# Attention with locality-sensitive hashing, then two feed-forward blocks: product with v in runs of three key blocks

## The chip, the cores and the metric

The kernel runs on one core of one Trainium2 chip. The metric is the device time of the program in microseconds; the smaller the better. The profile is of one execution, and its times count from the first instruction (the span).

## The reference

Inputs: q, k, v of shape (2, 8, 768, 64), `proj` (64, 6), and the weights of two feed-forward blocks. Everything is float32.

```python
q_bucket = sum over bits of ((q @ proj) > 0) * 2**bit      # k_bucket in the same way
mask = q_bucket[:, :, :, None] == k_bucket[:, :, None, :]
scores = where(mask, (q @ k.T) / sqrt(64), -1e9)
attn = exp(scores - max) / (sum + 1e-9)
x = (attn @ v), heads side by side                          # 1536 tokens x 512
h = x @ w_in;  x = (h * cos(h)) @ w_out                     # w_in 512 x 2048
out = (silu(x @ w_gate) * (x @ w_val)) @ w_out2             # w_gate, w_val 512 x 1536
```

## The kernel before

The instructions are issued in the order in which the program writes them; each engine has its own queue and works it off in that order, and waits on semaphores where data or a buffer is missing.

Attention works on 8 pairs of heads (`NPAIR`), two heads j = 0, 1 side by side. A pair has 6 blocks of 128 queries, so there are 48 units u (`NU`); three units make a half of the queries of a pair (384 queries), 16 halves (`NH`). The loop at L701 calls `att_step(u)` for each unit, and L723, L724 and L733 call it for five more steps (u = 48 to 52) in which the last units drain. One step works on three ages of units at once:

- for unit u: `mm_scores(u, j)` (L458) makes the scores of 128 queries against 768 keys: two matmuls over X and Y (L466) and two over Z and W (L468), which carry the hash bits and the low parts, into a PSUM tile `s` (two buffers). `row_max` (L471) on VectorE takes the tile to SBUF as `p` with its row minimum of the negated scores, `row_exp` (L482) on ScalarE makes the exponentials and their sums;
- for unit u - 1: `row_norm` (L491): VectorE makes the reciprocal `rv` of the sums (L493, L494) and POOL multiplies both `p` with it (L497);
- for unit u - 2: `p_transpose(u - 2, j, g, engine)` (L501), four times, for head j and half g of the keys: three 128x128 transposes on TensorE (L510) into a PSUM tile `t`, of which there are two (`ps_t`, L218), and one copy of the three into `pt`, by ScalarE (L516) in the calls (0, 0), (1, 0) and (1, 1), by VectorE (L518) in the call (0, 1);
- for a half whose three units are transposed: `av(half, kb)` (L522): the product of v with `pt` for key block kb = 0 to 5, one matmul for each head (L528), accumulated in the one PSUM tile `av` (`ps_v`). Each of these float32 matmuls shows as two instructions of 384 columns; v has 64 columns, so head 0 takes one half of the array's columns and head 1 the other. `av_close(half)` (L534) copies the finished tile to `xh` on ScalarE (L539) and puts what is left of it in `xl` on VectorE (L540).

In step u, `hv, kv = divmod(u - 5, HB)` with `HB` = 3 names the half and which of its three steps this is. Key blocks 2 kv and 2 kv + 1 come behind the first two calls of `p_transpose`, and `av_close` comes in the third step ahead of the last two calls.

In between, `fill("prep")` and `fill("build")` (L602) move two side jobs on by one piece. `prep` (L273) prepares q and k of the next pair in the first three units of a pair: transposes (L286), their copies (L292 on ScalarE, L296 on VectorE), casts (L300), the hash bits (L329, L335, L339), the low parts on POOL (L356), and the DMAs that place them, all on SP's queue. `build_early` (L169) takes one weight chunk of 64-bit floats to float32 in nearly every third unit: one copy on ScalarE (L137) and three steps on VectorE (L152, L156, L160).

After attention the first feed-forward block (L1055 on) and the second (L1111 on) run, with nearly all matmuls in `each_of_three` (L644).

Of the kernel before, what the change touches and what calls it, by code (L numbers as in the profile page):

```python
# [26 lines left out]
def lsh_attention_moe_moe2(  # L27
# [20 lines left out]
    NBLK = S // P  # L48
    HALF = S // 2
    HB = NBLK // 2  # L50
# [407 lines left out]
    def mm_scores(u, j):  # L458
        pr, i = divmod(u, NBLK)
        X, Y, Z, W = heads[pr]  # L460
        ps = ps_s.tile([P, 1024], F32, tag="s", name=f"s{u}_{j}")
        KZ = D + 2 * NB
        qs = slice(i * P, (i + 1) * P)
        cols = (slice(0, 512), slice(512, S))
        for ks in cols:
            nc.tensor.matmul(out=ps[:, ks], lhsT=X[:, j, qs], rhs=Y[:, j, ks], start=True, stop=False)  # L466
        for ks in cols:
            nc.tensor.matmul(out=ps[:, ks], lhsT=Z[:KZ, j, qs], rhs=W[:KZ, j, ks], start=False, stop=True)  # L468
        scores[u, j] = ps

    def row_max(u, j):  # L471
        ps = scores.pop((u, j))
        pt = pp.tile([P, S], F32, tag="p", name=f"p{u}_{j}")
        mn = sm.tile([P, 1], F32, tag="mn", name=f"mn{u}_{j}")
        nc.vector.tensor_scalar(  # L475
            out=pt, in0=ps[:, :S], scalar1=-MASKED, scalar2=None,
            op0=ALU.min, op1=ALU.min, accum_out=mn,
        )
        probs[u, j] = pt
        nbias[u, j] = mn  # L480

    def row_exp(u, j):  # L482
        pt = probs[u, j]
        if j == 0:
            sums[u] = sm.tile([P, 2], F32, tag="sv", name=f"sv{u}")
        nc.scalar.activation(  # L486
            out=pt, in_=pt, func=AF.Exp, bias=nbias.pop((u, j)), scale=-1.0,
            accum_out=sums[u][:, j : j + 1],
        )

    def row_norm(u):  # L491
        rv = sm.tile([P, 2], F32, tag="rv", name=f"rv{u}")
        nc.vector.tensor_scalar(out=rv, in0=sums.pop(u), scalar1=EPS, scalar2=None, op0=ALU.add)  # L493
        nc.vector.reciprocal(out=rv, in_=rv)  # L494
        for j in range(2):
            pt = probs[u, j]
            nc.gpsimd.tensor_scalar(  # L497
                out=pt, in0=pt, scalar1=rv[:, j : j + 1], scalar2=1.0, op0=ALU.mult, op1=ALU.mult
            )

    def p_transpose(u, j, g, eng):  # L501
        half, i = divmod(u, HB)
        if (half, j) not in pts:
            pts[half, j] = pv.tile([P, NBLK, HALF], F32, tag="pt", bufs=4, name=f"pt{half}_{j}")
        dst = pts[half, j]
        src = probs[u, j]
        ps = ps_t.tile([P, 512], F32, tag="t", name=f"t{u}_{j}_{g}")
        for c in range(HB):
            kb = g * HB + c
            nc.tensor.transpose(  # L510
                ps[:, c * P : (c + 1) * P], src[:, kb * P : (kb + 1) * P], ident
            )
        o = dst[:, g * HB : (g + 1) * HB, i * P : (i + 1) * P]
        s3 = ps[:, :HALF].rearrange("p (c t) -> p c t", c=HB)
        if eng == "act":
            nc.scalar.activation(out=o, in_=s3, func=AF.Copy)  # L516
        else:
            nc.vector.tensor_copy(o, s3)  # L518
# [3 lines left out]
    def av(half, kb):  # L522
        pr, hf = divmod(half, 2)
        if kb == 0:
            avs[half] = ps_v.tile([P, 512], F32, tag="av", name=f"av{half}")
        ps = avs[half]
        for j in range(2):
            nc.tensor.matmul(  # L528
                out=ps[j * D : (j + 1) * D, :HALF],
                lhsT=nat["v", pr][:, j, BLOCKS[kb], :], rhs=pts[half, j][:, kb, :],  # L530
                start=(kb == 0), stop=(kb == NBLK - 1),
            )

    def av_close(half):  # L534
        pr, hf = divmod(half, 2)
        ps = avs.pop(half)
        b, cc = divmod(pr, H // 2)
        sl = slice(b * S + hf * HALF, b * S + (hf + 1) * HALF)
        nc.scalar.activation(out=xh[:, cc, sl], in_=ps[:, :HALF], func=AF.Copy)  # L539
        nc.vector.tensor_tensor(  # L540
            out=xl[:, cc, sl], in0=ps[:, :HALF], in1=xh[:, cc, sl].bitcast(F32),
            op=ALU.subtract,
        )
        pts.pop((half, 0)), pts.pop((half, 1))
# [54 lines left out]
    NH = NPAIR * 2  # L599
    side = {"prep": iter(()), "build": iter(())}  # L600

    def fill(*what):  # L602
        for nm in what:
            next(side[nm], None)

    def att_step(u):


        hv, kv = divmod(u - 5, HB)
        live = u < NU  # L610
        tr = 0 <= u - 2 < NU
        if live:
            mm_scores(u, 0)
        if 0 <= u - 1 < NU:
            row_exp(u - 1, 1)
        if tr:
            p_transpose(u - 2, 0, 0, "act")
        if live:
            row_max(u, 0)
        if 0 <= u - 1 < NU:  # L620
            row_norm(u - 1)
        fill("prep")
        if tr:
            p_transpose(u - 2, 0, 1, "dve")
        if 0 <= hv < NH:
            av(hv, 2 * kv)
            av(hv, 2 * kv + 1)
        fill("prep", "build")
        if live:
            mm_scores(u, 1)  # L630
            row_exp(u, 0)
        if 0 <= hv < NH and kv == HB - 1:
            av_close(hv)
        if tr:
            p_transpose(u - 2, 1, 0, "act")
        if live:
            row_max(u, 1)
        fill("prep")
        if tr:
            p_transpose(u - 2, 1, 1, "act")  # L640
            probs.pop((u - 2, 0)), probs.pop((u - 2, 1))
        fill("prep", "build")
# [58 lines left out]
    for u in range(NU):  # L701
        pr, i = divmod(u, NBLK)
        if i == 0:
            side["prep"] = prep(pr + 1) if pr + 1 < NPAIR else iter(())
            if pr == 0:
                rest, second = first, side["prep"]
                order = (rest, rest, second, second, second, second, second, rest, rest)
                side["prep"] = itertools.chain((next(g) for g in order), second)
        if i == 4 and pr + 2 < NPAIR:
            load_pair(pr + 2, "qk")  # L710
        if i == 5 and 0 < pr < NPAIR - 1:
            load_pair(pr + 1, "v")
        if u + 3 in early_steps:
            fetch_next()
        if u in early_steps:
            side["build"] = build_early(early_steps.index(u))
        if u >= NU - 5 and u < NU - 1:
            split(*(uses[0] + uses[1] + uses[2])[u - NU + 5], pool=qk, tag="XYZW"[u - NU + 5], bufs=2)
        att_step(u)

    hps[0] = ps_p.tile([P, 512], F32, tag="pp", name="h0")
    side["prep"] = (hidden(hps[0], "in", 0, [a]) for a in range(NCC))
    att_step(NU)  # L723
    att_step(NU + 1)  # L724
    hps[1] = ps_t.tile([P, 512], F32, tag="t", name="h1")
    actx.close()
# [463 lines left out]
```

## Time and profile before

| | |
|---|---|
| device time, median of 3 runs | 797.24 us (795.46 to 798.85) |
| span of the profiled execution | 793.2 us (its own device time is not given apart from it) |
| instructions | 12687 |
| TensorE busy (matmuls) | 775.2 us, 98% |
| VectorE busy | 608.1 us, 77% |
| ScalarE busy | 516.3 us, 65% |
| POOL busy | 498.6 us, 63% |
| av matmuls (L528) | 384 instructions, starting from 35.4 to 252.5 us |

PE is TensorE's matmuls, PEld its weight loads, DVE is VectorE, ACT is ScalarE. The ends of matmuls are modelled and they overlap, so the distance between starts tells more than a length. Idle time of an engine that the others don't wait for costs nothing. A row that merges several instructions (x8) runs from the first one's start to the last one's end.

### The profile page before, as it was taken

To read this page: it belongs to the slowest core of one execution; us is meant where nothing else is said; L and a number is where in the kernel's file an instruction comes from. 1 tells how busy PE (TensorE), PEld (TensorE's weight loads), DVE (VectorE), ACT (ScalarE), POOL (GpSimd) and SP (SyncE) were. 2 spreads that over 40 slices of the span, in tenths; PEclk is the share of its full clock that TensorE was granted. 3 is DMA by queue.
4 is the path that set the end of the run, shared out by engine and by line. 5 is a ranking of instruction groups with operands and counts; after the bars stand their busy time and mean duration, and the time that the engine had idled before them with its cause. 6 is when DMAs were issued, how large, how long until landed. Compare 5 with 4: busy or idle time off the path is not lost. (4 is left out here: it accounts for less than half of the span.)

```text
span 793.2 us, 12687 instructions
## 1 busy us (share of the span) xinstructions
PE 775.2 (98%) x4100; PEld 634.3 (80%) x4100; DVE 608.1 (77%) x1121; ACT 516.3 (65%) x1009; POOL 498.6 (63%) x426
## 2 busy tenths in 40 slices
PE   6799999999999999999999999999999999999998
PEld 4666666666676788888888888889999989999996
DVE  6878888888774899988888799587777687655654
ACT  5778777777885888787778777744444445444432
POOL 4764565466463777767767988657655595655450
PEclk9999999999999999999999999999999999999999
DMA  3755756666413577878875756122122213412102
GB/s 119 192 132 150 202 133 174 173 139 165 126 41 115 181 241 235 263 251 289 294 229 189 254 194 224 40 68 67 54 81 66 80 27 126 141 42 79 41 1 79
DMA packets 72545, 113.01 MB, mean 142 GB/s; under 512 B 6656, under 2 KB 44704, under 8 KB 72480
## 3 DMA queue, kind: packets, MB, share of 16 engines
q1 hardware_dynamic: 72480, 112.21, 46.9%
q8 instruction: 32, 0.52, 0.3%
q14 instruction: 33, 0.27, 0.1%
HBM read 76.29 MB, written 18.35 MB: 119 GB/s over the span
## 5 line engine op out<-in xcount | busy, mean ns | idle before, releaser
L497 POOL TENSOR_SCALAR p<-p,rv 128x768 f32<-128x768 f32 x96 | 94.9, 1000 | 91.7 <-DVE rv L494 64.3
L475 DVE TENSOR_SCALAR_CACHE_REDUCE p<-s 128x768 f32<-128x768 f32 x96 | 91.1, 953 | 31.6 <-PE s L468 27.8
L486 ACT ACTIVATE p<-p,mn 128x768 f32<-128x768 f32 x96 | 89.8, 935 | 9.0 <-DVE p L475 4.9
L516 ACT ACTIVATE pt<-t 128x384 f32<-128x384 f32 x144 | 66.6, 486 | 41.3 <-PE t L510 41.1
L510 PE MATMUL t<-ident,p 128*128 128x128 f32 x576 | 85.0, 273 | 4.5 <-DVE pt L518 4.1
L510 PEld LDWEIGHTS t<-ident,p 128*128 128x128 f32 x576 | 67.5, 140 | 14.5 <-DVE pt L518 4.8
L528 PE MATMUL av<-pt,vn 128*64 128x384 f32 x384 | 72.1, 498 | 0.0
L930 ACT ACTIVATE uh<-u 128x384 fp32r<-128x384 f32 x48 | 23.8, 521 | 62.4 <-DVE u L925 62.4
L466 PE MATMUL s<-Y,X 128*128 128x512 f32 x192 | 58.8, 387 | 1.5 <-DVE X L389 1.5
L685 ACT ACTIVATE r<-r 128x512 f32<-128x512 f32 x48 | 30.4, 633 | 34.8 <-DVE r L677 34.7
L468 PE MATMUL s<-W,Z 76*128 76x512 f32 x192 | 50.2, 343 | 2.6 <-DVE Z L439 2.4
L466 PEld LDWEIGHTS s<-Y,X 128*128 128x128 f32 x192 | 29.0, 191 | 28.5 <-DVE rv L494 7.8
L673 DVE SCALAR_TENSOR_TENSOR rf<-ki,h 128x512 f32<-128x512 int32 x46 | 31.9, 693 | 20.4 <-ACT ki L670 20.0
L919 ACT ACTIVATE sg<-gate 128x384 f32<-128x384 f32 x36 | 18.9, 526 | 42.7 <-DVE gate L970 42.6
L137 ACT ACTIVATE w<-raw 128x512 f32<-128x512 f32 x68 | 44.7, 659 | 1.1 <-DMA raw<-in_moe_w_gate_dram 1.1
L646 PE MATMUL o<-out_1s,uh 128*128 128x512 f32 x144 | 44.9, 392 | 0.0
L646 PE MATMUL o<-out_0s,uh 128*128 128x512 f32 x144 | 44.9, 392 | 0.0
L528 PEld LDWEIGHTS av<-pt,vn 128*64 128x64 f32 x384 | 23.4, 136 | 25.8 <-issue 25.6
L697 DVE TENSOR_TENSOR g<-h,r 128x512 f32<-128x512 f32 x48 | 33.0, 687 | 13.0 <-ACT r L686 13.0
L156 DVE SCALAR_TENSOR_TENSOR bw<-w,bw 128x512 int32<-128x512 int32 x55 | 38.0, 691 | 2.4 <-ACT w L137 1.4
L152 DVE TENSOR_SCALAR bw<-raw 128x512 int32<-128x512 int32 x55 | 37.9, 689 | 0.6
L160 DVE SCALAR_TENSOR_TENSOR w<-raw,bw 128x512 int32<-128x512 int32 x55 | 37.5, 681 | 0.6
(1814 smaller groups left out, 2442.2 us busy)
## 6 DMA issues: line engine op xcount, KB each, us to landing
f<-w SPq DMA_DIRECT2D x58, 256.0 KB
raw<-in_moe_w_out_dram SPq DMA_DIRECT2D x28, 512.0 KB
raw<-in_moe_w_in_dram SPq DMA_DIRECT2D x16, 512.0 KB
raw<-in_moe_w_gate_dram SPq DMA_DIRECT2D x12, 512.0 KB
raw<-in_moe_w_val_dram SPq DMA_DIRECT2D x12, 512.0 KB
Y<-kH SPq DMA_DIRECT2D x28, 192.0 KB
vn<-in_v_dram SPq DMA_DIRECT2D x8, 384.0 KB
gate_0f<-f SPq DMA_DIRECT2D x12, 256.0 KB
```

Source lines behind the costliest of these rows:

```text
L137: nc.scalar.activation(out=t, in_=raws[i][:, :, 1].bitcast(F32), func=AF.Copy, scale=2.0**-112)
L152: nc.vector.tensor_scalar(out=sign, in0=high, scalar1=-(2**31), scalar2=None, op0=ALU.bitwise_and)
L156: nc.vector.scalar_tensor_tensor(out=word, in0=ti, scalar=3, in1=sign, op0=ALU.logical_shift_left, op1=ALU.bitwise_or)
L466: nc.tensor.matmul(out=ps[:, ks], lhsT=X[:, j, qs], rhs=Y[:, j, ks], start=True, stop=False)
L468: nc.tensor.matmul(out=ps[:, ks], lhsT=Z[:KZ, j, qs], rhs=W[:KZ, j, ks], start=False, stop=True)
L475: nc.vector.tensor_scalar(out=pt, in0=ps[:, :S], scalar1=-MASKED, scalar2=None, op0=ALU.min, op1=ALU.min, accum_out=mn,)
L486: nc.scalar.activation(out=pt, in_=pt, func=AF.Exp, bias=nbias.pop((u, j)), scale=-1.0, accum_out=sums[u][:, j : j + 1],)
L497: nc.gpsimd.tensor_scalar(out=pt, in0=pt, scalar1=rv[:, j : j + 1], scalar2=1.0, op0=ALU.mult, op1=ALU.mult)
L510: nc.tensor.transpose(ps[:, c * P : (c + 1) * P], src[:, kb * P : (kb + 1) * P], ident)
L516: nc.scalar.activation(out=o, in_=s3, func=AF.Copy)
L528: nc.tensor.matmul(out=ps[j * D : (j + 1) * D, :HALF], lhsT=nat["v", pr][:, j, BLOCKS[kb], :], rhs=pts[half, j][:, kb, :], start=(kb == 0) ...
L646: nc.tensor.matmul(out=out_ap, lhsT=s, rhs=m, start=first and i == 0, stop=last and i == 2, **flags)
```

## The change

The twelve matmuls of a half are made in two runs in place of three. In the first of the three steps (kv = 0) key blocks 0 to 2 are multiplied, at the old place behind the first two transposes; in the second step (kv = 1) key blocks 3 to 5, behind `row_max(u, 1)` and a piece of `prep`, between the third and the fourth call of `p_transpose`, and `av_close` follows at once. The third step has no product with v.

```diff
         if tr:
             p_transpose(u - 2, 0, 1, "dve")
-        if 0 <= hv < NH:
-            av(hv, 2 * kv)
-            av(hv, 2 * kv + 1)
+        if 0 <= hv < NH and kv == 0:
+            for kb in range(HB):
+                av(hv, kb)
         fill("prep", "build")
         if live:
             mm_scores(u, 1)
             row_exp(u, 0)
-        if 0 <= hv < NH and kv == HB - 1:
-            av_close(hv)
         if tr:
             p_transpose(u - 2, 1, 0, "act")
         if live:
             row_max(u, 1)
         fill("prep")
+        if 0 <= hv < NH and kv == 1:
+            for kb in range(HB, NBLK):
+                av(hv, kb)
+            av_close(hv)
         if tr:
             p_transpose(u - 2, 1, 1, "act")
```

## Rows read from the trace of the kernel before

**Rows 1.** The page, part 1: busy time of each engine, share, instructions.

```profile
PE 775.2 (98%) x4100; PEld 634.3 (80%) x4100; DVE 608.1 (77%) x1121; ACT 516.3 (65%) x1009; POOL 498.6 (63%) x426
```

**Rows 2.** Windows: length; busy us (count) PE, PEld, DVE, ACT, POOL; clock; DMA.

```profile
34.00:232.00 198.00, 197.42 (x1298) 137.40 (x1297) 161.84 (x374) 152.56 (x336) 113.63 (x108) 1.00 0.59 152
```

**Rows 3.** Waits of TensorE, 34 to 232 us: us in total, times, longest.

```profile
PE trq L286 <- DMA qn<-in_q_dram: 0.4, 1, 0.4
PE s L468 <- DMA W<-kT: 0.2, 1, 0.2
```

**Rows 4.** Timeline of TensorE's matmuls, units 27 and 28: start us, us, what.

```profile
139.78 0.82 PE L510 MATMUL t<-ident,p 128*128 128x128 f32 x6
140.53 1.51 PE L528 MATMUL av<-pt,vn 128*64 128x384 f32 x8
141.97 0.62 PE L466 MATMUL s<-Y,X 128*128 128x512 f32 x2
142.43 0.52 PE L468 MATMUL s<-W,Z 76*128 76x512 f32 x2
142.78 0.82 PE L510 MATMUL t<-ident,p 128*128 128x128 f32 x6
143.35 0.61 PE L466 MATMUL s<-Y,X 128*128 128x512 f32 x2
```

**Rows 5.** Timeline of TensorE's matmuls at the end of attention.

```profile
243.32 1.51 PE L528 MATMUL av<-pt,vn 128*64 128x384 f32 x8
244.76 0.88 PE L510 MATMUL t<-ident,p 128*128 128x128 f32 x6
...
248.85 4.09 PE L528 MATMUL av<-pt,vn 128*64 128x384 f32 x24
```

**Rows 6.** Timeline of VectorE, units 27 to 28.

```profile
144.47 0.68 DVE L160 SCALAR_TENSOR_TENSOR w<-raw,w 128x512 int32<-128x512 int32 x1
145.07 0.94 DVE L475 TENSOR_SCALAR_CACHE_REDUCE p<-s 128x768 f32<-128x768 f32 x1
...
145.95 0.16 DVE L493 TENSOR_SCALAR rv<-sv 128x2 f32<-128x2 f32 x1
...
146.22 0.54 DVE L518 COPY pt<-t 128x384 f32<-128x384 f32 x1
147.50 0.56 DVE L540 TENSOR_TENSOR xl<-av,xh 128x384 fp32r<-128x384 f32 x1 [0.74 <-ACT xh L539]
147.97 0.95 DVE L475 TENSOR_SCALAR_CACHE_REDUCE p<-s 128x768 f32<-128x768 f32 x1
```

**Rows 7.** Timeline of ScalarE, units 27 to 28.

```profile
140.62 0.49 ACT L516 ACTIVATE pt<-t 128x384 f32<-128x384 f32 x1
...
147.00 0.47 ACT L539 ACTIVATE xh<-av 128x384 fp32r<-128x384 f32 x1
...
148.96 0.94 ACT L486 ACTIVATE p<-p,mn 128x768 f32<-128x768 f32 x1 [0.41 <-DVE p L475]
```

**Rows 8.** Timeline of VectorE in unit 31, with preparation of the next pair.

```profile
160.47 0.56 DVE L300 CAST qH<-qT 128x768 fp32r<-128x768 f32 x1
160.95 0.55 DVE L296 COPY kT<-trk 128x384 f32<-128x384 f32 x1
```

**Rows 9.** Timeline of all engines in unit 4, a unit without av.

```profile
29.84 0.60 PE L466 MATMUL s<-Y,X 128*128 128x512 f32 x2
...
30.95 1.83 POOL L356 TENSOR_TENSOR kT<-kT,kH 128x768 f32<-128x768 f32 x1
...
31.72 1.09 DVE L493 TENSOR_SCALAR rv<-sv 128x2 f32<-128x2 f32 x1
...
32.92 0.54 DVE L518 COPY pt<-t 128x384 f32<-128x384 f32 x1
...
33.52 0.55 PE L510 MATMUL t<-ident,p 128*128 128x128 f32 x3 [0.95 <-DVE pt L518]
...
33.82 0.60 PE L466 MATMUL s<-Y,X 128*128 128x512 f32 x2
```

## The prediction, made before the change was run

> **What bounds the kernel now.** I read the engine shares first, then the windows by stage, then TensorE's waits, then its order of time inside the attention stage. TensorE is busy nearly all the time [rows 1]. In the stretch that the change touches, 34 to 232 us, it is busy 197.42 of 198 us at the full granted clock, 1.00, which is the 2.4 GHz level [rows 2], and it waits 0.6 us for anybody there, 0.4 for a load of q and 0.2 for W [rows 3]. So the stage runs at the rate at which TensorE can issue. VectorE is busy 161.84 us and ScalarE 152.56 us of the same 198 us [rows 2]: they follow with about a fifth of their time to spare. What the change takes from TensorE's stream shortens the kernel; any wait that it puts there lengthens it. The stages behind it are TensorE's too, so a shift goes through to the end.
>
> A matmul's length is no measure of its cost, since they overlap; I use the distance between starts. Three letters name units u by u mod 3: A (2), B (0), C (1). Before, each has two key blocks of av; afterwards A has three, B three (late, between its last two transposes), C none. S0, S1 are the two score products, T00 to T11 the four groups of three transposes, AV2 and AV3 two and three key blocks for both heads.
>
> **What is removed: changes between av and its neighbours.** Six transposes in front of scores take 142.78 to 143.35, 0.57 us; in front of av 139.78 to 140.53, 0.75. Av then takes until the scores start at 141.97, 1.44 [rows 4]. An AV2 between transposes and scores therefore costs 0.75 + 1.44 - 0.57 = 1.62 us. The same work in one long run is cheaper: 24 matmuls are 4.09 us long, 8 are 1.51 [rows 4, 5], so eight further pairs cost 2.58 us, 0.32 a pair. Four pairs are 1.29 us; the other 0.33 us is the change of kind. An AV3 in that place costs 1.62 + 0.64 = 2.26. Between two transposes (the late place) the trace has one case: av from 243.32, transposes at 244.76, again 1.44, and six transposes 0.88 long in place of 0.82 [rows 5]. It replaces six transposes at 0.11 each: 0.75 + 1.44 + 0.06 - 0.66 + 0.64 = 2.23. Per half: 3 x 1.62 = 4.86 before, 2.26 + 2.23 = 4.49 after, so 0.37 less. The last half's 24 matmuls stand in one run already [rows 5], which leaves 15 halves: 5.5 us saved (5.0 if only 0.33 goes each time).
>
> **What is moved: av_close.** Its copy xh (ScalarE) and difference xl (VectorE) come one unit earlier, behind the late AV3 of B. It issues no DMA and passes nothing on the queues of SP and POOL. But on ScalarE it now stands before B's last copy of transposes and C's first exponential, and on VectorE before the last step of the weight build (L160), C's first row maximum, the reciprocal (rv) and the copy of T01. That an xl holds those behind it is in the trace: VectorE stands idle 0.74 us for xh before the xl at 147.50, and the row maximum behind it starts only at 147.97 [rows 6].
>
> **What then limits C.** T11 can't start until VectorE has copied T01, since the transposes share two PSUM tiles. Time from the end of the late AV3 in B, with the handover of 0.06 us that rows 9 show between such a copy's end (32.92 + 0.54) and the transpose:
> TensorE starts T11 of B at -0.07 (1.44 against 1.51), S0 0.31 later (0.06 + 2 x 0.11 + 0.03), then 0.81 for scores, 0.57 for six transposes, 0.81 for scores [rows 4] and 0.33 for T10: it is ready for C's T11 at 2.76.
> VectorE: xh starts at 0.06 and xl 0.50 behind it (147.00 to 147.50), 0.47 to the next, L160 0.60 (144.47 to 145.07), row maximum 0.88, rv 0.27, copy 0.54 [rows 6, 7]: 3.32, so T11 starts at 3.38 and TensorE stands for 0.62 us. S0 is not late: it starts at 0.24 and is written 0.98 later (0.46 to the second product and its 0.52) [rows 4], before the row maximum at 1.63.
> With the preparation of the next pair (u mod 6 = 1, up to 37) VectorE also casts q, 0.48 from start to start, and copies one transposed k, about as long (0.55 against 0.56), before T01's copy [rows 8]; TensorE has two more groups of three transposes, 0.33 each: 0.62 + 0.96 - 0.66 = 0.92. Without a weight build (u = 40), ScalarE decides: the handover, xh, B's copy of T11 and the exponential that rv waits for, 0.06 + 0.47 + 0.49 + 0.94 [rows 7], let rv start at 1.96 in place of 2.51: 0.07 us.
> Units 7 to 46 hold 14 such C: six with preparation, seven without, one without a build: 6 x 0.92 + 7 x 0.62 + 0.07 = 9.9 us. A and B get longer on TensorE (4.38 to 5.0), which gives the other engines time to catch up; in B, today T10 (142.78) starts 1.67 us after ScalarE's copy of T00 has ended (140.62 + 0.49) with an AV2 between [rows 4, 7]; 1.62 us of that goes, and the 0.05 that is left is the handover, so I count no wait there. At the end, unit 49 has no av between its transposes: T10 waits for ScalarE's copy of T00, about 0.22 + 0.27 + 0.06 + 0.49 + 0.06 = 1.10 us after T00 starts, where two groups of transposes take 0.66: 0.4 us.
>
> The bounds of one such C. Below: nothing, if VectorE's chain overlaps more than its row spacings say; less than nothing is excluded, for TensorE has no wait there to lose. Above: the last unit that ran without av, u = 4, took 3.98 us from S0 to S0 (29.84 to 33.82), where TensorE's own work is 0.81 + 0.57 + 0.81 + 0.57 = 2.76: 1.22 lost, 0.95 of it at the very wait named above, T11 for T01's copy [rows 9]. There rv took 1.09 us and ended with a POOL instruction that began before it (30.95 + 1.83 = 32.78) [rows 9]; elsewhere it takes 0.16 [rows 6]. In the new C no such long POOL instruction stands beside rv, so I keep 0.62 and 0.92.
>
> **The sum.** 9.9 + 0.4 - 5.5 = +4.8 us, on a span of 793.2 us. The profile gives no time of its own for what lies around the span; the median of the runs, 797.24, is 4.0 above it, and I carry that over: 802.0 us.
>
> **The rivals.**
> Faster: the time in C is covered and only the changes of kind count: 797.2 - 5.5 = 791.7 us. It holds where VectorE's copy of T01 ends within 2.76 us of the av run, that is if its six steps take 0.6 us less than their spacing today. For it: VectorE has a fifth of idle time; against it: the steps are one queue, and it starts with a wait. The Trainium skill's "TensorEngine Tiling (Array Packing)", under Key Properties of its Tiling Modes, says that a change of tiling mode, not of the tile alone, drains TensorE. By that rule alone fewer changes are simply faster; the trace has the change at 0.33 us, and no run here shows yet that it is a drain.
> A wash: the waits in C are near 0.35 us each, half of what I reckon, because the chain's steps overlap somewhat: 14 x 0.35 + 0.4 - 5.5, about 797 us.
> Slower by more: C is as long as u = 4, since rv or the casts meet a POOL instruction: 14 x 1.22 + 0.4 - 5.5 = +12.0, 809.2 us. The Trainium skill's "SBUF — State Buffer" (Who interferes with whom) says that VectorE in a two-port mode and GpSimd exclude each other for a whole instruction; the rows with 1.09 us agree [rows 9].
>
> **How the numbers follow.** My forecast (797.5 to 806) gets 0.56, faster 0.14, the wash 0.15, slower by more 0.15. About 0.5%, 4 us, is what a measurement of this kernel can tell from no change. My forecast lies just above that bound: I give two thirds of its chance to slower and a third to no difference. Slower 0.38 + 0.15 = 0.53; same 0.18 + 0.15 = 0.33; faster 0.14. The range, 793 to 809, leaves out the faster case and the far end of the slowest one.
>
> **What would show it.** Right: among TensorE's waits between 34 and 232 us, about 13 for VectorE's copy of T01, 9 to 10 us together, where there are none now; av in runs of 12 matmuls, some 2.15 us long; units from S0 to S0 of about 5.0, 5.0 and 3.4 us, and 4.3 for a C with preparation. Wrong on the saving: the first transposes after the late av start later than 1.44 us after an equal AV2 would allow. Wrong on the wait: no such waits, C at 2.8 us. Wrong on its cause: the waits are for ScalarE's copies (T10) or for scores' PSUM. A C near 4.0 us with rv longer than 1 us would be the last rival.

## The result and the profile after

The changed kernel takes 803.29 us (median of 4 runs, 802.70 to 804.74); the kernel before took 796.88 us beside it (795.46 to 798.85). The ratio is 1.0090, with a 95% interval of 1.0073 to 1.0107: 6.4 us slower, where 4.8 were forecast (802.0 us).

The page's part 1 and the stretch of [rows 2] in the windows view, in the kernel after (columns as there):

```profile
PE 778.5 (97%) x4100; PEld 637.1 (79%) x4100; DVE 604.5 (75%) x1121; ACT 515.4 (64%) x1009; POOL 497.7 (62%) x426
...
34.00:232.00 198.00, 189.96 (x1255) 131.81 (x1254) 152.97 (x362) 145.21 (x323) 108.16 (x102) 1.00 0.59 151
```

TensorE, busy for 197.42 of these 198 us before [rows 2], is busy for 189.96 now, with the granted clock still at 1.00. The others are less busy too: nobody took more work, the stage goes slower. TensorE's waits from 34 to 240 us in the kernel after (us in total, times, longest), which answer to [rows 3]:

```profile
PE trk L286 <- DVE kT L296: 4.3, 6, 0.8
PE t L510 <- DVE pt L518: 2.2, 5, 0.4
PE s L468 <- DMA W<-kT: 0.5, 1, 0.5
PE t L510 <- POOL in2s L207: 0.5, 1, 0.5
PE t L510 <- POOL in0s L207: 0.4, 1, 0.4
PE trq L286 <- DMA qn<-in_q_dram: 0.3, 1, 0.3
```

The two DMA rows were there before. The first two are new, 6.5 us and eleven times, all for copies by VectorE. The two named L207 are new as well; they are taken up further down. TensorE's timeline in units 27 and 28 of the kernel after, which answers to [rows 4]:

```profile
147.12 2.16 PE L528 MATMUL av<-pt,vn 128*64 128x384 f32 x12
149.21 0.55 PE L510 MATMUL t<-ident,p 128*128 128x128 f32 x3
149.51 0.60 PE L466 MATMUL s<-Y,X 128*128 128x512 f32 x2
...
151.72 0.52 PE L510 MATMUL t<-ident,p 128*128 128x128 f32 x3
...
152.67 0.55 PE L510 MATMUL t<-ident,p 128*128 128x128 f32 x3 [0.43 <-DVE pt L518]
...
152.98 0.60 PE L466 MATMUL s<-Y,X 128*128 128x512 f32 x2
```

Unit 28 is a C: no av, 149.51 to 152.98, so 3.47 us long, and T11 (152.67) stands 0.43 us for VectorE. VectorE and ScalarE in the same unit, which answer to [rows 6, 7]:

```profile
149.33 0.49 ACT L539 ACTIVATE xh<-av 128x384 fp32r<-128x384 f32 x1 [1.09 <-PE av L528]
...
149.85 0.56 DVE L540 TENSOR_TENSOR xl<-av,xh 128x384 fp32r<-128x384 f32 x1 [0.34 <-ACT xh L539]
...
150.32 0.69 DVE L160 SCALAR_TENSOR_TENSOR w<-raw,w 128x512 int32<-128x512 int32 x1
...
150.94 0.94 DVE L475 TENSOR_SCALAR_CACHE_REDUCE p<-s 128x768 f32<-128x768 f32 x1
...
151.81 0.15 DVE L493 TENSOR_SCALAR rv<-sv 128x2 f32<-128x2 f32 x1
...
152.08 0.54 DVE L518 COPY pt<-t 128x384 f32<-128x384 f32 x1
```

From xl on VectorE has no gap: xl, the last step of the weight build, row maximum, rv, and only then the copy that T11 needs. The first of them waits for xh, and xh for the late av.

To see what a unit costs, take the distance from its first score product to the next unit's. Both tables below are made of such distances (us), for units 27 to 29 without preparation and for units with it (30 to 32; for B of the kernel before unit 24, since its unit 30 holds a DMA wait, and units 18 to 20 for build earlier and mixed, whose unit 30 is longer than their other ones):

| kernel | B, C, A without preparation | sum | B, C, A with preparation | sum |
|---|---|---|---|---|
| before | 4.36, 4.38, 4.36 | 13.10 | 5.01, 5.01, 5.30 | 15.32 |
| after | 5.10, 3.47, 5.01 | 13.58 | 5.63, 4.37, 5.96 | 15.96 |

A pair of halves takes 1.1 us more.

### The profile page after: what moved, and what is told of

It is laid out like the page before. It is cut to its first block, busy times and chain, and to the rows that moved or that the text cites. A ratio compares the mean times of both kernels' runs of the same rounds, so it can differ in the third digit from the quotient of the medians.

```text
span 803.0 us, 12681 instructions
## 1 busy us (share of the span) xinstructions
PE 778.5 (97%) x4100; PEld 637.1 (79%) x4100; DVE 604.5 (75%) x1121; ACT 515.4 (64%) x1009; POOL 497.7 (62%) x426
## 5 line engine op out<-in xcount | busy, mean ns | idle before, releaser
L510 PE MATMUL t<-ident,p 128*128 128x128 f32 x576 | 90.8, 280 | 7.0 <-DVE pt L518 4.5
L528 PE MATMUL av<-pt,vn 128*64 128x384 f32 x384 | 68.8, 494 | 0.0
L160 DVE SCALAR_TENSOR_TENSOR w<-raw,bw 128x512 int32<-128x512 int32 x55 | 37.4, 681 | 0.6
```

The costliest lines, as they stand in the source:

```text
L510: nc.tensor.transpose(ps[:, c * P : (c + 1) * P], src[:, kb * P : (kb + 1) * P], ident)
L528: nc.tensor.matmul(out=ps[j * D : (j + 1) * D, :HALF], lhsT=nat["v", pr][:, j, BLOCKS[kb], :], rhs=pts[half, j][:, kb, :], start=(kb == 0) ...
```

## The experiments

Six edits of the kernel after take single steps out of VectorE's queue in C or put one in; two measure a price in the kernel before; four more move the second run or another product. Units of each:

| kernel | us | ratio to before, 95% | B, C, A without preparation | B, C, A with preparation |
|---|---|---|---|---|
| six runs | 807.23 | 1.0144 (1.0127 to 1.0161) | 4.66 each | |
| build later | 806.51 | 1.0134 (1.0119 to 1.0149) | 5.10, 3.14, 5.01 | 5.63, 4.05, 7.17 |
| close later | 803.06 | 1.0087 (1.0072 to 1.0102) | 5.11, 3.14, 5.12 | 5.61, 4.18, 6.24 |
| both later | 809.84 | 1.0177 (1.0162 to 1.0192) | 5.10, 3.14, 5.12 | 5.61, 4.18, 7.50 |
| build earlier | 801.58 | 1.0066 (1.0046 to 1.0085) | 5.11, 3.14, 5.01 | 5.63, 4.05, 5.94 |
| and norm later | 804.68 | 1.0107 (1.0085 to 1.0130) | 5.10, 2.87, 5.34 | 5.63, 3.81, 7.28 |
| xl twice, after | 816.43 | 1.0252 (1.0227 to 1.0278) | 5.10, 4.05, 5.00 | 5.63, 4.96, 5.94 |
| xl twice, before | 798.74 | 1.0036 (1.0019 to 1.0052) | 4.36 to 4.38 | A 5.56 |
| second run in C | 795.43 | 0.9992 (0.9981 to 1.0004) | 3.23, 5.01, 5.01 | 3.39, 5.65, 5.94 |
| bits beside av | 794.22 | 0.9973 (0.9965 to 0.9982) | 4.38, 4.36, 4.36 | 5.03, 5.03, 5.16 |
| C and bits | 795.39 | 1.0000 (0.9991 to 1.0008) | 3.44, 5.01, 5.01 | 3.39, 5.65, 5.79 |
| mixed | 792.43 | 0.9957 (0.9944 to 0.9970) | 4.38, 4.36, 5.00 | 3.40, 5.66, 5.16 |

The kernel before took 795.7 to 796.1 us beside them (medians of 7 to 27 runs).

**Six runs: the price of a change of kind.** The kernel before, with each key block of a unit in a run of its own:

```diff
             av(hv, 2 * kv)
-            av(hv, 2 * kv + 1)
...
         fill("prep")
+        if 0 <= hv < NH:
+            av(hv, 2 * kv + 1)
+            if kv == HB - 1:
+                av_close(hv)
```

> The kernel before, but the two key blocks of a unit are taken apart: one at the old place, one between the last two groups of transposes; av_close follows the last one. Every unit has the same work as before, but each half of the queries has six runs of av in place of three. Theory (each change between av and its neighbours costs TensorE about 0.3 us): a single key block costs 1.62 - 0.65 = 0.97 us at the old place and 1.59 - 0.65 = 0.94 at the late one, so 5.73 a half in place of 4.86, 15 halves: 13 us more than the kernel before, about 810 us, with units of 4.65 us in place of 4.38. Rival (the distance between starts at the change is only how the profile shows it, and costs nothing): units stay at 4.38 us, about 797 us.

It took 807.23 us. TensorE's timeline of it:

```profile
149.50 0.49 PE L510 MATMUL t<-ident,p 128*128 128x128 f32 x3
149.92 0.87 PE L528 MATMUL av<-pt,vn 128*64 128x384 f32 x4
150.72 0.55 PE L510 MATMUL t<-ident,p 128*128 128x128 f32 x3
```

The units are 4.66 us where they were 4.37, with no wait in them: 0.29 for one more run, near the 0.33 of the sum. So the saving is real, and the kernel after did save it; its loss stands elsewhere.

**Build later.** Is L160 in C's queue what delays the copy? `fill("build")` falls away at the end of B's step, and so L160 is issued at the next place for a build, in the middle of C, behind the copy of T01:

```diff
             p_transpose(u - 2, 1, 1, "act")
...
-        fill("prep", "build")
+        fill("prep")
+        if u % HB:
+            fill("build")
```

> The changed kernel, but the last step of the weight build (L160) is issued in the middle of the third unit (C), behind VectorE's copy of T01, in place of the end of B. Theory (VectorE's queue behind the late av: xl, L160, row maximum, rv, copy of T01, holds C's T11): the copy of T01 comes up to 0.60 us earlier. In a C without preparation ScalarE's exponential then decides, as in unit 40 of the changed kernel, which had no build and took 3.14 us where the others took 3.47: 0.33 less, seven times. In a C with preparation, 4.37 us, the whole 0.60 goes, six times. Together 5.9 us less than the changed kernel: about 797.4 us, C at 3.1 and 3.8 us. Rival (C is short of time because of ScalarE's copies or because two PSUM tiles can't be passed on faster): C stays at 3.47 and 4.37 us, about 803.3 us.

C without preparation fell as expected, from 3.47 to 3.14, C with it by half of what was expected, from 4.37 to 4.05 (3.8), and the kernel is slower than the change: A with preparation went from 5.96 to 7.17. The timeline of VectorE, POOL and TensorE there, and the wait:

```profile
168.64 1.35 DVE L160 SCALAR_TENSOR_TENSOR w<-raw,w 128x512 int32<-128x512 int32 x1
...
169.41 2.24 POOL L356 TENSOR_TENSOR qL<-qT,qH 128x768 f32<-128x768 f32 x1
...
169.91 0.95 DVE L475 TENSOR_SCALAR_CACHE_REDUCE p<-s 128x768 f32<-128x768 f32 x1
...
170.78 0.55 DVE L296 COPY kT<-trk 128x384 f32<-128x384 f32 x1
...
171.39 0.52 PE L329 MATMUL pj<-qT,pjq 128*32 128x384 f32 x2 [1.17 <-DVE kT L296]
```

```profile
PE pj L329 <- DVE kT L296: 5.8, 5, 1.2
```

L160 takes 1.35 us here in place of 0.69, beside POOL (in C without preparation it takes 1.26, and nobody waits for it there); the row maximum and the copy of k stand behind it, and now the hash-bit product waits, 5.8 us in all. The copy of T01 was not the only one on that queue with somebody waiting for it.

**Close later, and both later.** The same question for xh and xl: `av_close` goes back to its old place in C, alone and together with the edit above.

```diff
+        if 0 <= hv < NH and kv == 2:
+            av_close(hv)
         if tr:
             p_transpose(u - 2, 1, 0, "act")
...
-            av_close(hv)
```

> The changed kernel, but av_close (xh and xl) is issued one unit later, at its old place in C ahead of T10; the runs of av stay. Theory: xh no longer stands before B's last copy and C's exponential on ScalarE, and xl and the wait for xh no longer stand before L160, the row maximum, rv and the copy of T01 on VectorE. L160 then runs while the late av does, the row maximum starts with its scores (about 1.3 us after the end of av in place of 1.63), and rv waits for the exponential (about 2.0): T11 at 2.9 to 3.0 in place of 3.4. C without preparation about 3.05 us in place of 3.47, with preparation about 3.9 in place of 4.37: 7 x 0.42 + 6 x 0.45 = 5.6 us less, about 797.7 us. Rival (the place of av_close is nothing; C is short because PE has no av in it): C stays as it is, about 803.3 us.

> Both moves together: L160 behind the copy of T01 in C, and av_close at its old place in C. Theory: what is left in front of C's T11 is ScalarE's copy of B's T11, its exponential, rv and the copy of T01: 0.06 + 0.49 + 0.94 + 0.27 + 0.54 and the handovers, about 2.5 us behind the end of av, where TensorE is ready at 2.76. C without preparation 2.8 to 2.95 us, with preparation 3.5 to 3.7. Against the changed kernel 7 x 0.6 + 6 x 0.75 = 8.7 us less: about 794.6 us, somewhat faster than the kernel before (796.9). If the two moves do the same thing twice, as the rival of one common limit on ScalarE would have it, this run gives what the better of the two single moves gives, about 797.5 us.

Close later: 803.06 us, no different from the change, where 797.7 was expected. C gained 0.33 and 0.19, but A lost 0.11 (T00 and T01 now wait for ScalarE's copies, which stand behind xh) and 0.28 with preparation (the hash-bit product again, 0.2 each time). Both later is the slowest of the three, 809.84 us: C is no shorter than with one of the two moved, since T10's wait for ScalarE (see the next kernels) is behind it, and in A the delays add up:

```profile
PE pj L329 <- DVE kT L296: 7.7, 6, 1.5
```

**Build earlier, and norm later.** The same step taken out of C the other way: in B, L160 ahead of the late av, where VectorE would only wait for xh. The second kernel also puts rv behind T01's copy in C.

```diff
         fill("prep")
+        if u % HB == 0:
+            fill("build")
         if 0 <= hv < NH and kv == 1:
...
-        fill("prep", "build")
+        fill("prep")
+        if u % HB:
+            fill("build")
```

```diff
-        if 0 <= u - 1 < NU:
+        if 0 <= u - 1 < NU and kv != 2:
             row_norm(u - 1)
...
             p_transpose(u - 2, 0, 1, "dve")
+        if 0 <= u - 1 < NU and kv == 2:
+            row_norm(u - 1)
```

> The changed kernel, but the last step of the weight build (L160) is issued ahead of the late av of B and of av_close, in place of behind them: VectorE does it while TensorE is in the late av, before POOL's long instructions of C. Theory now (C's T11 waits for VectorE's queue; L160 put into C only moved the wait, because the copy of the second transposed k is in the same queue and the product of the hash bits waits for it): C as in the run with L160 in C, 3.13 us without preparation and 4.05 with it, and nothing lost in the A behind it, 5.0 and 5.94 us. 5 x 0.34 + 6 x 0.32 = 3.6 us less than the changed kernel: about 799.6 us. Rival (what C gains its neighbours lose, whatever is moved, since VectorE's or ScalarE's work between two runs of av is the limit): A longer by as much, about 803 us.

> The run with L160 ahead of the late av, and in the units without av the reciprocal (row_norm, with POOL's two products) is issued behind VectorE's copy of T01, not ahead of it. Theory: what is left in front of T11 is scores written, row maximum, rv, copy of T01, one after the other: 1.08 + 0.88 + 0.28 + 0.54 + 0.06 = 2.84 us from S0, where TensorE needs 2.52. Without rv 2.56: C at about 2.85 us without preparation, 3.8 with it. 0.28 x 7 + 0.27 x 6 = 3.6 us less than with L160 moved alone: about 796.0 us, like the kernel before. POOL's products for the next unit come 0.5 us later, so T00 of the next unit may wait about 0.1 us for them. Rival (C's floor of 3.13 us is ScalarE's: its two exponentials and the copies): C stays at 3.13 and 4.05, about 799.6 us.

Build earlier is the best place found for L160 and brings 1.7 us of the 6.4 back (801.58): C falls by 0.33 and 0.32 and no A or B gets longer by it. Ten such C make 3.3 us, about what was expected; the medians show half of it, and why stays open. Its 3.14 has another cause: T10 starts 0.14 us behind ScalarE's copy of T00, so it waits for that one, and T11 then for 0.11 more. With rv behind the copy C fell to 2.87 and 3.81, as expected, without preparation to within 0.11 of what TensorE needs by itself (2.76; with preparation that is 3.42); but the kernel got slower, because the later rv makes POOL's products late for A:

```profile
PE t L510 <- POOL p L497: 7.3, 7, 1.1
```

Six of these waits are 1.1 us each, in the six A with preparation (the seventh is in unit 5, 0.6 us): more than the 0.3 a C saves. A without preparation got longer too, from 5.01 to 5.34.

**xl twice, after and before.** One extra xl (0.56 us, the same values again) in each of the two kernels:

```diff
+        for _ in range(2):
             nc.vector.tensor_tensor(
                 out=xl[:, cc, sl], in0=ps[:, :HALF], in1=xh[:, cc, sl].bitcast(F32),
...
```

> The changed kernel with xl computed twice in each av_close (the same values again). Theory: xl stands on VectorE in front of L160, the row maximum and the copy that C's T11 waits for, so 0.47 us more in each of 14 C: 6.6 us more than the changed kernel, about 809.8 us, C at 3.9 and 4.85 us. Rival (VectorE's queue is not what C waits for): C as in the changed kernel, about 803.2 us.

> The kernel before with xl computed twice in each av_close. Theory: there an AV2 stands between T01 and T11, the copy of T01 ends 0.6 us or more before T11, and the doubled xl stands behind that copy: units stay at 4.38 us, no more than 1 us in all, about 796 to 797 us. Rival (VectorE's work costs time in the kernel before as well): 16 x 0.47 = 7.5 us more, about 803.5 us.

The waits of the first, then of the second:

```profile
PE t L510 <- DVE pt L518: 8.0, 8, 1.6
PE trk L286 <- DVE kT L296: 7.6, 6, 1.4
```

```profile
PE pj L329 <- DVE kT L296: 1.1, 6, 0.2
```

The same 16 instructions cost 13.1 us after (816.43 against 803.29) and 2.9 before (0.36%). In the changed kernel ten of the fourteen C get longer by 0.58 to 0.63, the whole of the instruction: VectorE's queue behind the late av is the path that sets C. Units 7 and 40 grow by 0.31, and the last two C by 1.47 each, with T11 waiting 1.6 us for VectorE. That makes 9.5 us, more than the 6.6 expected; the rest of the 13.1 is not in these units and stays open (the two profiled executions are 9.8 us of span apart). In the kernel before VectorE's queue does not set C; from unit 5 to unit 47, waits for loads apart, only A with preparation shows the extra xl (5.56 against 5.30, six times), so that more than the 1 us of the expectation was lost.

**Second run in C.** If the loss is C's alone, two runs should be good where the unit behind a run has time. The kernel after, with the second run and `av_close` in the third step; B is now the unit without av.

```diff
-        if 0 <= hv < NH and kv == 0:
-            for kb in range(HB):
+        if 0 <= hv < NH:
+            for kb in {0: range(HB), 2: range(HB, NBLK)}.get(kv, ()):
                 av(hv, kb)
...
+        if 0 <= hv < NH and kv == HB - 1:
+            av_close(hv)
...
-        if 0 <= hv < NH and kv == 1:
-            for kb in range(HB, NBLK):
-                av(hv, kb)
-            av_close(hv)
```

> Two runs of three key blocks as in the changed kernel, but the second run stands in the third unit (C) at the old place behind T01, and av_close behind it at the place that it had before; so B is the unit without av. Theory (the loss comes of what stands on VectorE's queue in the unit that is emptied, xl and L160 in C; the saving of 0.37 us a half is real): B has no xl, and L160 stands at its end, behind its copy of T01. There T11 waits 0.3 to 0.5 us for that copy behind row maximum and rv: B about 3.2 us, C and A 5.0. A half without preparation about 13.2 us (before 13.1, changed kernel 13.6). With preparation B has the three copies and two copies of q on ScalarE, and C's T00 and T01 wait some 0.4 us for them: 3.4 + 6.0 + 5.94 = 15.4 (before 15.3, changed kernel 15.9). About 0.2 us a pair more than the kernel before: 797.5 us, 6 us less than the changed kernel. Rival (any unit without av loses what the changed kernel loses, wherever it is): about 803 us.

795.43 us (expected 797.5): with the same number of changes between av and its neighbours, all of the 6.4 us is back. B is 3.23 without preparation, so 0.47 above TensorE's own 2.76; with preparation it is 3.39, and two more groups of transposes, 0.33 each, bring TensorE's own work from 2.76 to 3.42: nothing is lost there.

**Bits beside av.** What else changes kind? In the kernel before the hash-bit product (L329, 32 columns) stands among transposes in the third preparing unit. Here it stands right ahead of av:

```diff
-        fill("prep")
+        beside = live and u > NBLK and u % NBLK == 2
+        if not beside:
+            fill("prep")
         if tr:
             p_transpose(u - 2, 0, 1, "dve")
+        if beside:
+            fill("prep")
```

> The kernel before, but in the unit with the product of the hash bits (u mod 6 = 2, from u = 8) that piece of preparation is issued behind T01 instead of ahead of it, so that its eight matmuls of 32 columns stand directly ahead of av's of 64 columns. Theory (it is the change between transposes or scores and products with few columns that costs): one change less in each of six pairs, 0.3 us each, the unit 5.0 us in place of 5.30: 1.8 us less than the kernel before, about 794.2 us. Rival (32 and 64 columns are two kinds, and the change between them costs as well): no difference, about 796 us.

```profile
162.86 0.82 PE L510 MATMUL t<-ident,p 128*128 128x128 f32 x6
163.61 0.52 PE L329 MATMUL pj<-qT,pjq 128*32 128x384 f32 x2
...
163.97 0.49 PE L329 MATMUL pj<-kT,pjk 128*32 128x384 f32 x2
164.39 1.51 PE L528 MATMUL av<-pt,vn 128*64 128x384 f32 x8
```

The time is the expected one, 794.22 us, but the working behind it was not: A shrank by 0.14 us, not 0.3. From the last L329 to av there are still 0.42 us, where pairs within a run follow each other at 0.32 to 0.37: going from 32 to 64 columns costs something too. Six units make 0.8 of the 1.7 us between the medians; where the rest is from stays open.

**C and bits, and mixed.** Both edits together, and then both where the unit lengths say that they pay: two runs only in the six halves whose empty B has preparation (its two groups of transposes are of q, where the expectation says keys). The diff shows the runs of mixed; the edit of bits beside av goes with it.

```diff
-            av(hv, 2 * kv)
-            av(hv, 2 * kv + 1)
+            two_runs = hv % 2 == 0 and hv < NH - 4
+            runs = {0: range(HB), 2: range(HB, NBLK)} if two_runs else {}
+            for kb in runs.get(kv, () if two_runs else (2 * kv, 2 * kv + 1)):
+                av(hv, kb)
```

> Both: the second run of three key blocks in C, and the product of the hash bits directly ahead of av. Theory: the sum of the two, 797.5 - 1.8 = 795.7 us, within the noise of the kernel before (796). Rival: either part fails as told for it, 797.5 us or 801 us and more.

> The kernel before, with the hash-bit product's preparation piece issued behind T01 in the third preparing unit of a pair of halves (as in e10_bits_beside_av), and with two runs of three key blocks, in the third unit (A) and in the second (C) of a half, the first unit (B) left without, in those six halves only whose first unit prepares keys; the other halves keep three runs of two. Worked out from unit lengths of e10 and e11: the pair of halves is then 3.40 (B without a run, with preparation) + 5.65 (C) + 5.15 (A) + 4.37 + 4.37 + 5.01 = 27.95 us, against the kernel before's 28.42, so 0.47 less in each of six pairs, 2.8 us: about 793.1 us, 0.35% below the kernel before, if the gain of leaving a run out is there in each half where the emptied unit has other work for TensorE. Rival: the C unit with its three-block run and preparation, or the first unit of the half behind, pays the gain back (a wait of the T products for the copies of VectorE), and the time is no better than e10's 794.2; if the empty unit costs what it did in the halves without preparation there, it is about 795.4.

C and bits gives 795.39 us. That is the expected time, but not by the expected sum: it is no better than second run in C alone (795.43) and worse than bits beside av alone (794.22). A got shorter by 0.15, and B without preparation longer by 0.21 (3.44 against 3.23): in five of these B T11 waits for VectorE, 0.34 to 0.66 us each, the loss of the kernel after in another unit. Mixed has no such unit. TensorE's waits in it, and its timeline of a C and an A with preparation:

```profile
PE t L510 <- DVE pt L518: 0.9, 1, 0.9
PE t L510 <- ACT pt L516: 0.3, 1, 0.3
```

```profile
156.49 2.16 PE L528 MATMUL av<-pt,vn 128*64 128x384 f32 x12
158.58 0.62 PE L466 MATMUL s<-Y,X 128*128 128x512 f32 x2
...
160.29 0.60 PE L466 MATMUL s<-Y,X 128*128 128x512 f32 x2
...
162.62 1.51 PE L528 MATMUL av<-pt,vn 128*64 128x384 f32 x8
```

The first wait is in unit 4, as in the kernel before [rows 9], the second in unit 48, where the kernel before has one of 0.34 us too.

792.43 us (12 runs; 17 of the kernel before, 796.13), ratio 0.9957 (0.9944 to 0.9970). This is the fastest of all the kernels here: 3.7 us below the kernel before and 10.9 below the change, by the medians. A pair of halves measures 27.96 us, against the 27.95 it was built on and 28.42 before; six pairs make 2.8 of the 3.7 us, and the rest stays open.

## Why the prediction was right, point by point

**What bounds the stage.** Right: TensorE had no slack, and the waits put there came out in the time, though not each to the microsecond. The unit lengths show that directly; the place of the second run, with av_close behind it, is the only difference between 803.3 and 795.4 us.

**The saving.** Right, at its lower value. TensorE's own work in a half is 5.01 + 5.00 + 2.76 = 12.77 us against 13.10: 0.33 saved, where the sum took 0.37 and allowed 0.33. The runs of 12 take 2.16 us (2.15 forecast). Six runs gives 0.29 for one change. The Trainium skill's "TensorEngine Tiling (Array Packing)", Key Properties, says that a change of tiling mode drains TensorE; the 0.29 agrees with a price for the change, and no run here shows that it is a drain. By that rule alone the kernel would have been faster, and it was not.

**The wait in C.** Right in mechanism, in place and nearly in size: 0.71 lost without preparation (3.47 against 2.76; 0.62 forecast), and with it a unit of 4.37 us (4.3 forecast). xl twice and build earlier show the cause, the one moving C by the whole length of an instruction, the other by half of one. One detail was off: with preparation the wait isn't at T11. VectorE and TensorE there:

```profile
166.27 0.56 DVE L300 CAST qH<-qT 128x768 fp32r<-128x768 f32 x1
...
166.75 0.55 DVE L296 COPY kT<-trk 128x384 f32<-128x384 f32 x1
...
167.22 0.55 DVE L518 COPY pt<-t 128x384 f32<-128x384 f32 x1
167.35 0.55 PE L286 MATMUL trk<-ident,kn 128*128 128x128 f32 x3 [0.78 <-DVE kT L296]
...
167.74 0.49 PE L510 MATMUL t<-ident,p 128*128 128x128 f32 x3
```

The second group of k's transposes stands ahead of T11 and waits for the copy of the first group (166.75 + 0.55), which is on the same queue just ahead of T01's. So the waits came in two kinds, six and five, not as 13 of one kind, and as 6.5 us, not 9 to 10. The view counts idle time from the modelled end of the matmul before, so a wait row holds less than the unit loses (0.43 of the 0.71 in unit 28).

**What was missed.** "I count no wait there", of T10 in B, was wrong: the step took 0.06 us, VectorE's handover, for that of ScalarE. Where T10 waits for ScalarE's copy of T00 it starts 0.14 to 0.15 after the copy's end, in B and also in C. In unit 27, a B, the copy ends at 146.53 and T10 starts at 146.68:

```profile
146.04 0.49 ACT L516 ACTIVATE pt<-t 128x384 f32<-128x384 f32 x1
...
146.68 0.52 PE L510 MATMUL t<-ident,p 128*128 128x128 f32 x3
```

That is the 0.10 us by which B without preparation is longer than A (5.10 against 5.01), and the floor of 3.14 in C; so unit 40, the one without a build, lost 0.38 us where 0.07 was forecast. And the last pair of heads loses 1.92 of the 7.9 us by which the stretch from unit 5 to unit 47 is longer: 28.12 us against 26.20 in units 41 to 46: there the waits named L207 stand, 0.4 and 0.5 us, in units in which the splits of the next stage's weights (L205 on ScalarE, L207 on POOL) queue between the copies. The sum had these units at the price of the others (twice 0.25). The kernel before has the same splits in its units 43 to 46 and loses nothing there. No run took the splits away, so that cause is read, not tested.

**The sum.** Too small. 4.8 us were forecast; the medians show 6.4, and 7.2 to 7.6 if the kernel before is taken as it ran beside the later kernels (795.7 to 796.1). From unit 5 to unit 47, which holds 14 of the 15 halves, the forecast is 9.9 - 14 x 0.37 = 4.7 us, and the two traces show 7.9. Three terms make up 3.0 of the 3.2 us between them: the saving at 0.33 a half (0.6 us), the C, which lost 11.1 us in place of 9.9, and the B, at nothing in the sum, which lost 1.2 (0.10 in six units, 0.62 in unit 45). At the end of attention the wait was as forecast (T10 of unit 49 stands for 0.34 us, 0.4 in the sum).

The two profiled executions lie further apart, by 9.8 us of span (793.2 to 803.0): 1.4 of that arises before unit 5, where both kernels do the same. After's own execution lies 1.7 us above its span, where the prediction carried over 4.0. A later execution of the kernel before with the same span of 793.2 took 795.01 us, so the span came from a quick execution and the median from slower ones. The 2.3 us too much in that term stand against a shift that was too small: that 802.0 lies within 1.3 us of the measured time is in part luck.

**The rivals.** Faster: excluded by the unit lengths of C. A wash: C would have been near 3.1, as in build earlier, which even then is 1.0066. Slower by more: C near 4.0 with a long rv; rv takes 0.15 [rows 9 had 1.09]. The rival by a POOL neighbour did show up, though in an edit and for another instruction (L160, 1.35 us).

## What to carry to other kernels

A matmul that moves takes its eviction with it, so before merging runs look at the unit that is left short: on each engine that feeds it, add up what is queued between the moved eviction and the copy for which TensorE waits next. Where the sum is longer than TensorE's own work, leave another unit empty, one with work of its own (mixed), and not the one right behind the eviction. Taking one step out of a full queue helps only where the next one in need of that queue, or of the next engine, has time: four of five reliefs in C were paid back in the unit behind.

## What the runs showed of the hardware

L160 (both operands in SBUF) took 0.68 us with POOL idle [rows 6] and 0.69 in the kernel after, but 1.35 beside POOL in build later; POOL's L356 beside it took 2.24, against 1.82 to 1.84 in the kernel before (1.83 in [rows 9]). The Trainium skill's "SBUF — State Buffer" (Who interferes with whom) says that a VectorE instruction with two inputs in SBUF contends with a GpSimd instruction that reads there; these rows agree. Moving a step in time can so double it.

TensorE's clock early in the program differs from execution to execution. Windows of the executions before and then after (length; busy us of the engines; granted clock third from the end):

```profile
24.00:28.00 4.00, 2.71 (x20) 2.46 (x20) 3.34 (x8) 3.04 (x8) 3.58 (x4) 1.00 1.11 205
28.00:32.00 4.00, 2.72 (x20) 2.19 (x18) 3.49 (x8) 2.95 (x8) 3.61 (x4) 1.00 0.65 138
```

```profile
24.00:28.00 4.00, 1.76 (x6) 1.58 (x7) 2.92 (x8) 2.23 (x5) 3.32 (x6) 0.71 1.12 209
28.00:32.00 4.00, 4.00 (x19) 3.81 (x17) 2.70 (x7) 2.40 (x6) 3.61 (x4) 0.50 0.53 96
```

A granted clock of 0.50 is the 1.2 GHz level. In the kernel after TensorE was at it from 28 to 32 us, and in the 4 us ahead of that, at 0.71, it was busy for 1.76; in the kernel before, busy for 2.71 and 2.72, it kept 1.00 in both windows. Over the first 34 us that is 0.80 against 0.95, and unit 5 starts at 35.23 us in place of 33.82. "xl twice, before", which is the kernel before but for one instruction per half, also has 0.80 and 35.24: this is no effect of the change.
